# Window attention feeding a routed expert layer: transposes by half arrays, value sums among them, a bank of its own for gate and route, 1e-9 inside the product

## The chip, the cores and the metric

The kernel runs on one core of a Trainium2 chip. The metric is the device time of one execution in microseconds (us). TensorE is called PE here (PEld is its weight load, which overlaps PE), VectorE DVE, ScalarE ACT, GpSimd POOL, and SP is the engine that issues most transfers.

## What is computed

Attention with a window of 16 and block summaries, whose output goes token by token to one of 8 experts. Cut to what matters (B=4, H=8, S=768, D=64; E=8 experts, DM=512, DF=1024):

```python
k_sum = k.reshape(B, H, nb, block, D).max(axis=3)      # block = 32, nb = 24
v_sum = v.reshape(B, H, nb, block, D).mean(axis=3)
scores_l_m = np.where(mask_l, scale * q @ k.T, -1e9)   # |i - j| < 16
scores_s = scale * q @ k_sum.T + np.log(block)
a = np.exp(scores_all - scores_all.max(-1))            # both kinds side by side
a = a / (a.sum(-1) + 1e-09)
x = a @ np.concatenate([v, v_sum])
...
e = argmax(x @ w_gate) if s == 0 or sigmoid(x @ w_local) < 0.5 else prev_e
p = softmax(x @ w_gate)
out[b, s] = p[e] * (np.maximum(x @ w1[e], 0) @ w2[e])
```

## The kernel before

**Attention.** A loop of 32 iterations, G = 0 to 31. One G is half the sequence (three blocks of 128 queries) of one pair of heads, two G make a pair of heads, eight G a batch. A query block meets 96 windowed keys and 24 summaries, so a score row has 120 entries. Iteration G works on three different G at once:

- `s_mm(G)` (L281, L287): mask and scores into one of two score tiles of two PSUM banks each, on 64x64 pieces of the array;
- `t_stage(G-2)` (L312, L313): six transposes of the exponentials, 128 rows x 120 columns each, three into each of two banks, and an ACT copy of each bank into `pt`;
- `sum_v` (L252, L254), once per pair of heads: a transpose of the value sums `va` into a third bank, and an ACT copy into `vs`, which POOL spreads into `vw` (L259);
- `s_max(G)` on DVE (L294), `s_exp(G)` on ACT (L302, six instructions);
- `a_mm(G-3)` (L323): the product with the values; `a_norm(G-3)` on DVE (L334 adds 1e-9, L335 takes the reciprocal, L336 multiplies).

PSUM has eight banks: four for scores, one for `a_mm`, and three that go round under the name "t". Transposes of all kinds, and the small matmuls of the routing, take the next of the three.

**Gate and route.** When a batch's attention is done, `x_rows_in` (L511, L518) transposes its rows for the gate: two blocks of 128 rows in each of three iterations (G = 10 to 12 for the first batch, 18 to 20, 26 to 28 for the next), four 128x128 transposes and one ACT copy per block into `hs`. `x_logits` (L528) makes the gate's logits of three blocks with 12 matmuls, ACT copies them (L532), PE turns them back (L535), DVE stores them (L537). Its results lie in columns of the score tile that the scores leave free (`self.spare`, L289, L525). Two iterations later `route` starts: a chain of some 30 small DVE steps with four stops on PE (L569, L575, L581, L602 to L605), which `small` (L458) places one or a few at a time between the steps of the loop.

**Experts.** From iteration 31 on the expert layer's matmuls (L1128 to L1130, L1158 to L1160) take PE. The last G's `t_stage`, `a_mm` and the last batch's gate and route are put among them by hand (`tail`).

**Loads.** SP issues, in program order, k, q, v and the windowed values `vw` of the coming pairs of heads, the stores of finished rows and the first expert's weights. An issue waits until the buffer's last reader is done, and all behind it wait too.

Of the kernel before, what the change touches and what calls it, by code (L numbers as in the profile page):

```python
# [19 lines left out]
P = 128  # L20
# [4 lines left out]
W = WL + NB  # L25
NU = S // P
# [27 lines left out]
XT = (0, 0, 1, 1, 2, 2)  # L54
XG = (2, 3)

# [16 lines left out]
class Kernel:  # L73
    def __init__(self, ctx, tc, qT, kT, vT, vW, maskc, identc, wgc, w1, w2, c32c, cb16c, out):
        self.tc, self.nc, self.out = tc, tc.nc, out
        self.steps, self.credit, self.have_p, self.last, self.early_in = [], 0, 0, None, {}
        self.calls = 0
# [6 lines left out]
        self.ps = {n: pool("ps_" + n, k, space=psum) for n, k in (("t", 3), ("a", 1))}  # L84
# [5 lines left out]
        self.spare = None  # L90
# [54 lines left out]
    def bank(self, which):  # L145
        if which == "a" and "a2" in self.ps:
            self.turn ^= 1
            which = "a2" if self.turn else "a"
        if which == "s":
            which = next(self.order)  # L150
        return self.ps[which].tile([P, 512], F32, name="b" + which[0])

    def free_banks(self):
# [4 lines left out]
        self.order = cycle(("s0", "s1", "s1"))  # L158


    def attention(self, tick, rows, tail):
        nc, tc, ident = self.nc, self.tc, self.ident
        with ExitStack() as ctx:
# [13 lines left out]
            vts, kss, vas, vss = {}, {}, {}, {}  # L177
# [17 lines left out]

            for t in kp:
                nc.vector.memset(t[:, 0:16], 0.0)
                nc.vector.memset(t[:, 16 + S:], 0.0)
# [22 lines left out]
            def reduce_v(n, v=None):  # L221
                va = vas[n] = wk.tile([P, NB], F32, name="va")
                nc.vector.tensor_reduce(out=va, in_=by32(vts.pop(n)) if v is None else v, op=ALU.add, axis=AX.X)

            def fold_v(n):
                f = by32(wk.tile([P, S // 2], F32, name="vf", bufs=1), 16)
                v = by32(vts.pop(n))
                for i in range(0, NB, NB // 2):
                    p = slice(i, i + NB // 2)
                    nc.gpsimd.tensor_tensor(out=f[:, p], in0=v[:, p, 0:16], in1=v[:, p, 16:32], op=ALU.add)  # L230
                folded[n] = f
# [18 lines left out]

            def sum_v(n, m):
                nc.tensor.transpose(out=m[:NB], in_=vas.pop(n), identity=ident)  # L252
                vs = vss[n] = wk.tile([NB, P], F32, name="vs", bufs=2)
                nc.scalar.copy(out=vs, in_=m[:NB])  # L254
# [11 lines left out]
            def s_mm(G):  # L266
# [22 lines left out]
                self.spare = sp[:, :, NG * W:]  # L289
# [7 lines left out]
            def s_exp(G):  # L297
                sp, nm = live[G]
                pr = wk.tile([P, 2, NG, W], F32, name="pr")
                for h in range(2):  # L300
                    for u in range(NG):
                        nc.scalar.activation(out=pr[:, h, u, :], in_=sp[:, h, u, :], func=AF.Exp,  # L302
# [3 lines left out]
            def t_stage(G):  # L306
                pr = live[G]
                pt = wk.tile([W, 2, NG, P], F32, name="pt", bufs=2)
                for h in range(2):
                    tp = self.bank("t")  # L310
                    for u in range(NG):
                        nc.tensor.transpose(out=tp[:W, P * u:P * u + P], in_=pr[:, h, u, :], identity=ident)  # L312
                    nc.scalar.copy(out=pt[:, h].rearrange("p u q -> p (u q)"), in_=tp[:W, 0:NG * P])  # L313
                live[G] = pt

            def a_mm(G):
# [3 lines left out]
                for u in range(NG):  # L320
                    for h in range(2):
                        for c in range(2):
                            nc.tensor.matmul(out=ap[64 * c:64 * c + 64, u, h, :], lhsT=pt[:, h, u, 64 * c:64 * c + 64],  # L323
                                             rhs=vw[n % 3][0:W, 2 * (NG * g + u) + c, h, :], start=True, stop=True)

            def a_norm(G):
# [7 lines left out]
                nc.vector.tensor_scalar(out=dn, in0=ap[:, :, :, D:D + 1], scalar1=1e-9, scalar2=None, op0=ALU.add)  # L334
                nc.vector.reciprocal(out=dn, in_=dn)  # L335
# [16 lines left out]
            for G in range(last_g):  # L352
# [10 lines left out]
                if LT <= G:  # L363
                    t_stage(G - LT)
                if G > 2 * GP and G % GP == 0 or G == 2 * GP + 1:
                    sum_v(G // GP, self.bank("t")[:, 0:P])
                if G in (2, 4):
                    sum_v(G // 2 - 1, self.bank("t")[:, 0:P])
# [57 lines left out]
            self.spare = None  # L426
# [31 lines left out]
    def small(self, n, pe=False):  # L458
# [3 lines left out]
        while self.credit > 0:  # L462
            heads = [h for h in list(self.steps)[:2] if h[0] not in ON_PE or pe and h[2] <= self.calls - ON_PE[h[0]]]
# [8 lines left out]
    def step(self, head):  # L472
        kind = head[0]
        self.last = head
# [8 lines left out]
        if head[0] is None:  # L483
            self.steps.remove(head)

# [8 lines left out]
    def flow(self, dt):  # L494

        self.t += dt
        while True:
            heads = [h for h in self.steps[:2]
                     if (h[3] <= self.t if h[0] in ON_PE or h[0] == "WAIT" else max(h[3], self.q) <= self.t + AHEAD)]
# [13 lines left out]

    def x_rows_in(self, b, u):

        m = self.x_transpose(b, u, "t")
        xt = self.hs[b, u] = self.mw.tile([P, 512], F32, name=f"hs{u % 4}")
        self.nc.scalar.copy(out=xt, in_=m)  # L518

    def x_logits(self, b, g):  # L520
# [4 lines left out]
        m = self.bank("t") if self.spare is None else self.spare[:, 0]  # L525
        for c in range(KT):
            for j, u in enumerate(us):
                nc.tensor.matmul(out=m[32 * j:32 * j + 32, 0:P], lhsT=self.wg[:, c], rhs=self.hs[b, u][:, P * c:P * c + P],  # L528
# [3 lines left out]
        nc.scalar.copy(out=l4, in_=m[0:32 * NG, 0:P])  # L532
        yield
        m = self.bank("t") if self.spare is None else self.spare[:, 1 - g]
# [3 lines left out]
                              in_=m[:, 0:32 * NG].rearrange("p (u e) -> p u e", u=NG)[:, :, 0:G9])  # L538


    def route(self, b):
# [26 lines left out]
        m = self.bank("t")  # L568
# [3 lines left out]
        v.tensor_tensor_scan(out=pm, data0=m[0:NU, 0:P], data1=self.zero[0:NU, 0:P], initial=0.0, op0=ALU.max, op1=ALU.max)  # L572
        yield "PE late" if b == 0 else "PE"
        m = self.bank("t")
# [1008 lines left out]
```

## Time and profile before

| | |
|---|---|
| time, median of 3 runs | 441.0 us (439.19 to 441.19) |
| the profiled execution | 438.48 us, of which 436.7 us are the span of the core |
| mean granted TensorE clock | 0.994 of full speed |
| PE busy | 416.0 us, 95% of the span |
| ACT, DVE, POOL busy | 201.4, 245.2, 214.0 us |
| DMA | 95.84 MB, mean 219 GB/s |

The page cuts the span into 40 slices of 10.9 us and gives the busy share of each in tenths. Attention is the first eleven slices, the experts are the rest. Times of rows are counted from the span's start.

### The profile page before, as it was taken

To read this page: it belongs to the slowest core of one execution; us is meant where nothing else is said; L and a number is where in the kernel's file an instruction comes from. 1 tells how busy PE (TensorE), PEld (TensorE's weight loads), DVE (VectorE), ACT (ScalarE), POOL (GpSimd) and SP (SyncE) were. 2 spreads that over 40 slices of the span, in tenths; PEclk is the share of its full clock that TensorE was granted. 3 is DMA by queue.
4 is the path that set the end of the run, shared out by engine and by line. 5 is a ranking of instruction groups with operands and counts; after the bars stand their busy time and mean duration, and the time that the engine had idled before them with its cause. 6 is when DMAs were issued, how large, how long until landed. Compare 5 with 4: busy or idle time off the path is not lost. (4 is left out here: it accounts for less than half of the span.)

```text
span 436.7 us, 12169 instructions
## 1 busy us (share of the span) xinstructions
PE 416.0 (95%) x4470; PEld 363.0 (83%) x4470; DVE 245.2 (56%) x609; ACT 201.4 (46%) x457; POOL 214.0 (49%) x305
## 2 busy tenths in 40 slices
PE   7799989989999999999999999999999999999992
PEld 6577878768898798998989889798988898978981
DVE  5776788888875798955522222215545732264720
ACT  4888878686955125512111112115454821266610
POOL 3688675778622313932021310304939883088930
PEclk9999999999999999999999999999999999999997
DMA  8999979999342670293092264200765794039771
GB/s 317 374 377 395 409 282 363 372 395 368 102 149 95 238 292 2 80 389 111 2 377 113 79 229 183 75 27 25 262 202 183 305 344 182 24 96 383 267 258 52
DMA packets 24006, 95.84 MB, mean 219 GB/s; under 512 B 2894, under 2 KB 3536, under 8 KB 19312
## 3 DMA queue, kind: packets, MB, share of 16 engines
q1 hardware_dynamic: 19328, 80.30, 48.9%
q0 software_dynamic: 4448, 14.29, 9.5%
q8 instruction: 42, 0.69, 0.7%
q14 instruction: 44, 0.36, 0.3%
q10 hardware_dynamic: 144, 0.20, 0.1%
HBM read 82.20 MB, written 12.71 MB: 217 GB/s over the span
## 5 line engine op out<-in xcount | busy, mean ns | idle before, releaser
L1158 PE MATMUL bs<-xT,h 128*128 128x256 f32 x352 | 101.4, 288 | 0.0
L1159 PE MATMUL bs<-xT,h 128*128 128x256 f32 x352 | 99.7, 283 | 0.0
L1160 PE MATMUL bs<-xT,l 128*128 128x256 f32 x352 | 99.5, 283 | 0.0
L1097 POOL DMA_INDIRECT xg<-x_dram,gidx x30 | 33.4, 1114 | 89.7 <-POOLq L1400 39.8
L1091 POOL TENSOR_TENSOR l<-stg,h 128x256 fp32r<-128x256 f32 x72 | 64.9, 935 | 15.0 <-ACT h L1083 14.7
L1128 PE MATMUL ba<-h,hT 128*128 128x512 f32 x176 | 71.5, 406 | 0.4
L1164 ACT ACTIVATE hT<-bs 128x512 fp32r<-128x512 f32 x44 | 26.3, 598 | 96.7 <-PE bs L1160 93.3
L1130 PE MATMUL ba<-h,hT 128*128 128x512 f32 x176 | 68.9, 392 | 0.0
L1129 PE MATMUL ba<-l,hT 128*128 128x512 f32 x176 | 68.7, 391 | 0.0
L1158 PEld LDWEIGHTS bs<-xT,h 128*128 128x128 f32 x352 | 67.4, 192 | 1.3 <-issue 0.8
L1166 DVE SCALAR_TENSOR_TENSOR hT<-bs,hT 128x512 fp32r<-128x512 f32 x44 | 30.4, 691 | 67.9 <-ACT hT L1164 57.1
L1159 PEld LDWEIGHTS bs<-xT,h 128*128 128x128 f32 x352 | 67.5, 192 | 0.4
L1160 PEld LDWEIGHTS bs<-xT,l 128*128 128x128 f32 x352 | 67.4, 192 | 0.0
L302 ACT ACTIVATE pr<-bs,nm 128x120 f32<-128x120 f32 x192 | 51.2, 358 | 8.8 <-DVE nm L294 6.4
L1083 ACT CAST h<-stg 128x1024 fp32r<-128x1024 f32 x48 | 48.9, 1052 | 9.2 <-PE ba L1130 8.2
L1144 POOL DMA_INDIRECT out_dram<-yo,sidx x24 | 26.4, 1102 | 47.4 <-ACT yo L1143 9.6
L1086 DVE TENSOR_TENSOR l<-stg,h 128x1024 fp32r<-128x1024 f32 x30 | 39.6, 1331 | 13.2 <-ACT h L1083 10.4
L1128 PEld LDWEIGHTS ba<-h,hT 128*128 128x128 f32 x176 | 33.1, 188 | 7.5 <-ACTq L1400 0.6
L1130 PEld LDWEIGHTS ba<-h,hT 128*128 128x128 f32 x176 | 33.0, 188 | 7.3
L1129 PEld LDWEIGHTS ba<-l,hT 128*128 128x128 f32 x176 | 33.2, 189 | 5.6
L259 POOL COPY vw<-vs 24x384 f32<-24x384 f32 x64 | 30.5, 518 | 8.5 <-ACT vs L254 6.1
L313 ACT COPY pt<-bt 120x384 f32<-120x384 f32 x64 | 27.8, 493 | 10.1 <-PE bt L312 10.1
(274 smaller groups left out, 665.1 us busy)
## 6 DMA issues: line engine op xcount, KB each, us to landing
stg<-in_w SPq DMA_DIRECT2D x28, 1024.0 KB, 7.0
vw<-in_vW SPq DMA_DIRECT2D x16, 780.0 KB, 7.9
few_w<-in_w SPq DMA_DIRECT2D x8, 1024.0 KB, 8.9
kp<-in_kT SPq DMA_DIRECT2D x16, 384.0 KB, 6.8
q<-in_qT SPq DMA_DIRECT2D x16, 384.0 KB, 7.3
vt<-in_vT SPq DMA_DIRECT2D x16, 384.0 KB, 7.6
x_dram<-xs SPq DMA_DIRECT2D x8, 768.0 KB, 5.4
wst<-in_w SPq DMA_DIRECT2D x8, 512.0 KB, 6.4
```

What stands on the lines that cost most here:

```text
L259: nc.gpsimd.tensor_copy(out=vw[n % 3][WL:W, t:t + NW // 4, :, 0:D], in_=vs.to_broadcast([NB, NW // 4, 2, D]))
L302: nc.scalar.activation(out=pr[:, h, u, :], in_=sp[:, h, u, :], func=AF.Exp, bias=nm[:, h, u:u + 1], scale=1.0)
L1083: self.nc.scalar.copy(out=hi, in_=src)
L1086: eng.tensor_tensor(out=lo, in0=src, in1=hi.bitcast(F32), op=ALU.subtract)
L1091: eng.tensor_tensor(out=lo[:, p], in0=src[:, p], in1=hi[:, p].bitcast(F32), op=ALU.subtract)
L1097: self.nc.gpsimd.indirect_dma_start(out=t, out_offset=None, in_=rows, in_offset=bass.IndirectOffsetOnAxis(ap=self.gidx[:, i:i + 1], axis=0))
L1128: nc.tensor.matmul(out=ps, lhsT=ah, rhs=wh, start=first, stop=False)
L1129: nc.tensor.matmul(out=ps, lhsT=ah, rhs=wl, start=False, stop=False)
L1130: nc.tensor.matmul(out=ps, lhsT=al, rhs=wh, start=False, stop=last)
L1158: nc.tensor.matmul(out=ps[:, j], lhsT=wh, rhs=xh, start=(k == 0), stop=False)
L1159: nc.tensor.matmul(out=ps[:, j], lhsT=wh, rhs=xl, start=False, stop=False)
L1160: nc.tensor.matmul(out=ps[:, j], lhsT=wl, rhs=xh, start=False, stop=(k == KT - 1))
```

## The change

- **Halves.** A transpose of 128 rows becomes two of 64 rows each, on the upper and the lower half of the array's rows, side by side. Each half writes a bank of its own, so a set of transposes holds two banks at once. `t_stage` becomes 12 half transposes and two ACT copies (one a bank), each of six blocks of 64 columns. The gate's transposes are done so too (`x_two`: 16 half transposes and two copies for two blocks of rows).
- **Value sums among them.** `va` is a seventh source in the same set: two more half transposes, and the copies are seven blocks long. `vs` and its copy are gone, POOL reads the sums from `pt`.
- **Banks.** The pool "t" has two banks instead of three. The third is "m", for `x_logits`, `route` and what follows it; a step holds it until its result is read (`own_m`, `free_m`), and others wait in program order. After the loop "t", "t" and "m" go round together. `self.spare` is gone.
- **Order.** The second `x_logits` of a batch moves behind `s_exp` of its iteration (`XSTEPS`).
- **1e-9.** `vw` gets a row with 1e-9 in the column of the denominators, the exponentials a 121st column of ones; DVE's addition is gone.
- The value sums' folding on POOL is done in place, and `pr` and `va` are fixed tiles.

```diff
-        self.ps = {n: pool("ps_" + n, k, space=psum) for n, k in (("t", 3), ("a", 1))}
+        self.ps = {n: pool("ps_" + n, k, space=psum) for n, k in (("t", 2), ("m", 1), ("a", 1))}
...
-XT = (0, 0, 1, 1, 2, 2)
+XT = (0, 1, 2)
 XG = (2, 3)
+XSTEPS = (((0, 2), (0, 4), (1, 2), (1, 3)), ((0, 0), (0, 1), (1, 2), (1, 3)))
...
-            def t_stage(G):
+            def t_stage(G, n=None):
                 pr = live[G]
-                pt = wk.tile([W, 2, NG, P], F32, name="pt", bufs=2)
-                for h in range(2):
-                    tp = self.bank("t")
-                    for u in range(NG):
-                        nc.tensor.transpose(out=tp[:W, P * u:P * u + P], in_=pr[:, h, u, :], identity=ident)
-                    nc.scalar.copy(out=pt[:, h].rearrange("p u q -> p (u q)"), in_=tp[:W, 0:NG * P])
-                live[G] = pt
+                pt = live[G] = wk.tile([WE, 2 * NG + 1, P], F32, name="pt", bufs=3)
+                srcs = [pr[:, h, u, :] for h in range(2) for u in range(NG)]
+                if n is not None:
+                    srcs.append(vas[n % 3])
+                    vss[n] = pt[0:NB, 2 * NG, :]
+                self.halves(srcs, WE, pt[:, 0:len(srcs)])
...
-                nc.vector.tensor_scalar(out=dn, in0=ap[:, :, :, D:D + 1], scalar1=1e-9, scalar2=None, op0=ALU.add)
-                nc.vector.reciprocal(out=dn, in_=dn)
+                nc.vector.reciprocal(out=dn, in_=ap[:, :, :, D:D + 1])
...
+    def halves(self, srcs, m, dst):
+        half = P // 2
+        n = len(srcs)
+        banks = [self.bank("t")[:m, 0:half * n].rearrange("p (i q) -> p i q", q=half) for c in range(2)]
+        for i, src in enumerate(srcs):
+            for c in range(2):
+                r = slice(half * c, half * c + half)
+                self.nc.tensor.transpose(out=banks[c][:, i], in_=src[r], identity=self.ident[r, r])
+        for c in range(2):
+            self.nc.scalar.copy(out=dst[:, :, half * c:half * c + half], in_=banks[c])
...
+    def own_m(self, who):
+        if self.rest:
+            return
+        while self.m_owner not in (None, who):
+            assert self.m_owner is not self
+            self.step(self.m_owner)
+        self.m_owner = who
...
-        m = self.bank("t") if self.spare is None else self.spare[:, 0]
+        self.own_m(self)
+        m = self.bank("m")
```

What moves on ACT, first batch, from the exponentials of G = 10 to the `pt` copies of iteration 14 (`pr` are exponentials, `hs` the gate's rows, `l` its logits, `vs` the value sums). Before:

```order
30 L302 ACTIVATE pr<-bs,nm 128x120 x6
31 L518 COPY hs_885<-bt 128x512
32 L518 COPY hs_892<-bt 128x512
33 L313 COPY pt<-bt 120x384 x2
34 L302 ACTIVATE pr<-bs,nm 128x120 x6
35 L518 COPY hs_963<-bt 128x512
36 L518 COPY hs_970<-bt 128x512
37 L532 COPY l_1001<-bs 96x128
38 L313 COPY pt<-bt 120x384 x2
39 L254 COPY vs<-bt 24x128
40 L302 ACTIVATE pr<-bs,nm 128x120 x6
43 L532 COPY l_1100<-bs 96x128
```

And now:

```order
25 L306 ACTIVATE pr_160<-bs,nm 128x120 x6
26 L538 COPY hs_906<-bt 128x8x64 x2
27 L538 COPY pt<-bt 121x6x64 x2
28 L306 ACTIVATE pr_161<-bs,nm 128x120 x6
29 L538 COPY hs_994<-bt 128x8x64 x2
30 L569 COPY l_1045<-bm 96x128
31 L538 COPY pt<-bt 121x7x64 x2
32 L306 ACTIVATE pr_160<-bs,nm 128x120 x6
33 L538 COPY hs_1101<-bt 128x8x64 x2
34 L538 COPY pt<-bt 121x6x64 x2
35 L306 ACTIVATE pr_161<-bs,nm 128x120 x6
36 L569 COPY l_1204<-bm 96x128
```

The copies of the gate's rows still stand behind the exponentials and ahead of the `pt` copies; the `vs` copy is gone, and the second copy of logits has moved behind the exponentials.

On PE, iteration 10, from its scores on (`va` the value sums, `xs` the rows for the gate). Before:

```order
207 L287 MATMUL bs<-kb_141,q_139 64x120 x12
208 L312 MATMUL bt<-ident,pr 120x128 x6
209 L252 MATMUL bt<-ident,va 24x128
210 L323 MATMUL ba<-vw_147,pt 64x65 x12
211 L511 MATMUL bt<-ident,xs 128x128 x8
```

And now:

```order
207 L292 MATMUL bs<-kb_144,q_142 64x120 x12
208 L536 MATMUL bt<-ident,pr_160 121x64 x12
209 L536 MATMUL bt<-ident,va_156 121x64 x2
210 L326 MATMUL ba<-vw_150,pt 64x65 x12
211 L536 MATMUL bt<-ident,xs 128x64 x16
```

The places stay; each transpose has become two with half the output columns.

## Rows read from the trace of the kernel before

**Rows 1.** The page's 40 slices of 10.9 us: busy tenths of PE and DMA, and GB/s.

```profile
PE   7799989989999999999999999999999999999992
...
DMA  8999979999342670293092264200765794039771
GB/s 317 374 377 395 409 282 363 372 395 368 102 149 95 238 292 2 80 389 111 2 377 113 79 229 183 75 27 25 262 202 183 305 344 182 24 96 383 267 258 52
```

**Rows 2.** Timeline of PE, iterations 11 to 14 (start us, us, engine, line, ...).

```profile
39.05 0.87 PE L312 MATMUL bt<-ident,pr 128*120 128x128 f32 x6
39.85 0.92 PE L323 MATMUL ba<-vw,pt 120*64 120x65 f32 x24
40.71 1.09 PE L511 MATMUL bt<-ident,xs 128*128 128x128 f32 x8
...
42.62 1.07 PE L528 MATMUL bs<-hs,wg 128*32 128x128 f32 x24
43.62 0.87 PE L312 MATMUL bt<-ident,pr 128*120 128x128 f32 x6
...
48.72 0.87 PE L312 MATMUL bt<-ident,pr 128*120 128x128 f32 x6
...
50.37 0.35 PE L281 MATMUL bs<-me 64*64 64x360 bf16 x4
```

**Rows 3.** Timeline of ACT in the same iterations.

```profile
36.92 1.57 ACT L302 ACTIVATE pr<-bs,nm 128x120 f32<-128x120 f32 x6
38.39 1.04 ACT L518 COPY hs<-bt 128x512 f32<-128x512 f32 x2
39.69 0.86 ACT L313 COPY pt<-bt 120x384 f32<-120x384 f32 x2 [0.26 <-PE bt L312]
...
41.91 1.13 ACT L518 COPY hs<-bt 128x512 f32<-128x512 f32 x2
...
44.26 0.86 ACT L313 COPY pt<-bt 120x384 f32<-120x384 f32 x2 [0.25 <-PE bt L312]
...
46.64 1.04 ACT L518 COPY hs<-bt 128x512 f32<-128x512 f32 x2
...
49.35 0.86 ACT L313 COPY pt<-bt 120x384 f32<-120x384 f32 x2 [0.27 <-PE bt L312]
...
52.89 1.56 ACT L302 ACTIVATE pr<-bs,nm 128x120 f32<-128x120 f32 x6
```

**Rows 4.** Groups by form, 0 to 130 us (count | busy us, mean ns | idle before).

```profile
L313 ACT COPY pt<-bt 120x384 f32<-120x384 f32 x64 | 27.8, 493 | 10.1 <-PE bt L312 10.1
...
L312 PE MATMUL bt<-ident,pr 128*120 128x128 f32 x192 | 27.6, 280 | 0.0
...
L334 DVE TENSOR_SCALAR dn<-ba 128x6 f32<-128x6 f32 x32 | 5.0, 157 | 5.4 <-PE ba L323 5.3
```

**Rows 5.** Waits, 0 to 130 us: who <- for whom, us in total, times, longest.

```profile
ACT pr L302 <- DVE nm L294: 6.4, 9, 2.5
...
DVE nm L294 <- ACT l L532: 4.1, 2, 2.2
...
PEld bt L312 <- issue: 3.4, 20, 0.2
PEld bt L569 <- ACT pt L313: 2.7, 2, 1.4
...
PEld bt L581 <- ACT pt L313: 0.6, 1, 0.6
```

**Rows 6.** Timeline of PEld where turned logits, not scores, precede the transposes.

```profile
111.04 0.66 PEld L312 LDWEIGHTS bt<-ident,pr 128*120 128x120 f32 x6
```

**Rows 7.** Timeline of DVE and PE in iteration 31, where the experts begin.

```profile
115.27 1.29 DVE L1103 TENSOR_TENSOR xT<-bt,xT 128x512 fp32r<-128x512 f32 x2 [0.40 <-ACT xT L1101]
...
115.69 0.87 PE L312 MATMUL bt<-ident,pr 128*120 128x128 f32 x6
116.32 0.36 PE L1158 MATMUL bs<-xT,h 128*128 128x256 f32 x1
```

More of the change, by code (lines that the diff above doesn't have):

```diff
@@ L150, in bank @@
             which = next(self.order)
+        if which in ("t", "m") and self.rest:
+            which = next(self.rest)
         return self.ps[which].tile([P, 512], F32, name="b" + which[0])
@@ L158, in free_banks @@
         self.order = cycle(("s0", "s1", "s1"))
+        while self.m_owner:
+            self.step(self.m_owner)
+        self.rest = cycle(("t", "t", "m"))
     def attention(self, tick, rows, tail):
@@ L176, in attention @@
             eye2, mask2 = me[:, 0:64], me[:, 64:]
-            vts, kss, vas, vss = {}, {}, {}, {}
+            vts, kss, vss = {}, {}, {}
+            vas = [cst.tile([P, WE], F32, name=f"va{i}") for i in range(3)]
             def load_k(n):
@@ L194, in load_w @@
                 nc.sync.dma_start(out=vw[n % 3], in_=self.vW[b, p])
+            for t in vas:
+                nc.gpsimd.memset(t, 0.0)
+            prs = [cst.tile([P, 2, NG, WE], F32, name=f"pr{i}") for i in range(2)]
+            for t in prs:
+                nc.gpsimd.memset(t[:, :, :, W:WE], 1.0)
             for t in kp:
@@ L462, in small @@
         while self.credit > 0:
-            heads = [h for h in list(self.steps)[:2] if h[0] not in ON_PE or pe and h[2] <= self.calls - ON_PE[h[0]]]
+            heads = [h for h in list(self.steps)[:2] if h[0] not in ON_PE or pe and h[2] <= self.calls - ON_PE[h[0]] and self.m_owner is not self]
             if not heads:
@@ L473, in step @@
         kind = head[0]
+        if kind in ON_PE:
+            self.own_m(head)
         self.last = head
@@ L512, in x_transpose, with hs_of, x_two @@
         return m
+    def halves(self, srcs, m, dst):
[8 more added lines that the diff above has]
+            self.nc.scalar.copy(out=dst[:, :, half * c:half * c + half], in_=banks[c])
+    def hs_of(self, b, u):
+        if (b, u // 2) not in self.hs:
+            self.hs[b, u // 2] = self.mw.tile([P, 2, KT, P], F32, name=f"hs{u // 2 % 2}")
+        return self.hs[b, u // 2][:, u % 2]
     def x_rows_in(self, b, u):
         m = self.x_transpose(b, u, "t")
-        xt = self.hs[b, u] = self.mw.tile([P, 512], F32, name=f"hs{u % 4}")
-        self.nc.scalar.copy(out=xt, in_=m)
+        self.nc.scalar.copy(out=self.hs_of(b, u).rearrange("p k t -> p (k t)"), in_=m)
+    def x_two(self, b, u):
+        self.hs_of(b, u)
+        srcs = [self.xs[b, v // NG][:, v % NG, P * c:P * c + P] for v in (u, u + 1) for c in range(KT)]
+        self.halves(srcs, P, self.hs[b, u // 2].rearrange("p j k t -> p (j k) t"))
     def x_logits(self, b, g):
@@ L532, in x_logits @@
         nc.scalar.copy(out=l4, in_=m[0:32 * NG, 0:P])
+        self.free_m()
         yield
-        m = self.bank("t") if self.spare is None else self.spare[:, 1 - g]
+        self.own_m(self)
+        m = self.bank("m")
         nc.tensor.transpose(out=m[:, 0:32 * NG], in_=l4, identity=self.ident[0:32 * NG, 0:32 * NG])
@@ L757, in early @@
         yield "PE"
-        m = self.bank("t")
+        m = self.bank("m")
         for t in range(n):
@@ L1329, in run @@
             g0 = GP * NP * b + GP * NP + 2
-            for u in range(NU):
-                at(g0 + XT[u], 1, self.x_rows_in, b, u)
+            for i in range(NU // 2):
+                at(g0 + XT[i], 1, self.x_two, b, 2 * i)
             for g in range(GP):
-                for G, i in ((0, 2), (0, 4), (1, 2), (1, 3)):
+                for G, i in XSTEPS[g]:
                     at(g0 + XG[g] + G, i, tiles, self.x_logits, b, g)
```

68 lines of the change are left out of this document (36 added, 32 removed).

## The prediction

> **What bounds the kernel now.** I read the page's slices first. From the eleventh slice on PE is at 9 almost throughout [rows 1]: that is the expert layer, PE's alone, and the change leaves its order of matmuls as it is. So what attention gains or loses up to the first expert matmul at 116.3 us [rows 7] is gained or lost at the end. Within attention the reader should see two things in the slices: PE stands at 7 to 9, and DMA is at 9 in eight of the first ten slices, at 282 to 409 GB/s [rows 1]. Loads are in flight nearly all the time, so an iteration that merely waits less for PE will soon wait for its keys or values. The timelines come next, for iterations 11 to 14, where the first batch's rows go through the gate. There PE runs without a gap: transposes, product, gate transposes, logits follow at once [rows 2]. ACT sits close behind: exponentials, gate copies, then a short wait of about 0.26 us for the transposes, `pt` copies, exponentials [rows 3]. Last the waits: where `route` runs, ACT waits for DVE and PE for ACT's `pt` copies [rows 5].
>
> **The half transposes.** Six full ones take 0.87 us [rows 2], one 0.28 [rows 4], so one follows another by (0.87 - 0.28) / 5 = 118 ns. The trace has no half transpose. Near bound: `a_mm`, which runs on two column halves at a time, issues 24 instructions in 0.92 us [rows 2], (0.92 - 0.28) / 23 = 28 ns apart. Far bound: if the two halves run one after the other, half the columns give 59 ns. I take 30 ns, from the nearer kind of work. Then a set of 12 takes 0.28 + 11 x 0.03 = 0.61 us instead of 0.87, one of 14 takes 0.67, and the gate's 16 take 0.73 instead of 1.09 [rows 2]. PE saves 0.26 us 32 times and 0.36 us nine times.
>
> **The copies.** ACT used to start its first `pt` copy 0.64 us after the transposes began (39.05 to 39.69) [rows 2, 3], since it needed three of them. Now both copies need the whole set: 0.61 + 0.12 = 0.73 us, with sums 0.79. So ACT sees the transposes 0.1 to 0.15 us later, although PE is done earlier. The `vs` copy saved goes against two copies that are a sixth longer than 493 ns [rows 4]; I count nothing for the pair.
>
> **Iterations without gate work.** PE's saving there has the loads behind it [rows 1]; 0, between -0.26 us an iteration and +0.15.
>
> **Two banks instead of three, in the gate's iterations.** This is the largest term. A set holds both "t" banks. After `x_two` they are free only when ACT has read both, and ACT does that behind the exponentials. Today one of three banks was free, and `t_stage` began at 39.05 while the gate copies ran until 38.39 + 1.04 = 39.43 [rows 2, 3]. Then it can begin at 39.55, `pt` copies at 40.28 instead of 39.69: +0.6. In iteration 12 the gate copies so run from 42.5 to 43.65, and the logits, which started at 42.62 [rows 2] with one block copied, need both copies now, as each writes half of each block: 43.75, `pt` copies at 45.5 instead of 44.26 [rows 3], +1.25. In iteration 13 the gate copies end at 48.95, `t_stage` starts at 49.05 instead of 48.72 [rows 2], `pt` copies at 49.8 instead of 49.35 [rows 3]; the logits come behind it now, which regains 0.8 on ACT. But PE still has 1.0 us of logits and 0.85 of `a_mm` to do, so the next scores start near 51.4 instead of 50.37 [rows 2], and the exponentials of iteration 14 at 54.2 instead of 52.89 [rows 3]: **+1.3 us**. In the second and third stretch the exponentials that start the chain wait for DVE already [rows 5], which hides part; I take +0.4 each. Sum +2.1, each stretch between +1.3 and -1.7 (what PE would save there if banks never bound: three gate sets of 0.36, two or three of 0.26).
>
> **Route in a bank of its own.** PE waited 2.7 us in two places (L569) and 0.6 in one (L581) for ACT to read a "t" bank [rows 5]; the "m" bank is free there. Behind it stand `a_mm` and the next scores. Between 0 and -3.3; I take -2.4, since in one iteration ACT's exponentials are what ends last anyway. The steps forced early by `own_m` change no place on PE in the loop: 0. The scores' tile no longer carries logits, so the 4.1 us in which the row maximum waited for the logits' copy [rows 5] go; the `pt` copies still end later there, 0.
>
> **1e-9 in the product.** 32 additions of 157 ns on DVE go [rows 4], 5.0 us of busy time. It counts where ACT waited for DVE's maximum, nine times [rows 5]: one addition each in eight of them, **-1.3**; between 0 and -2.6 (two each).
>
> **Array modes.** Where scores on 64x64 pieces precede the transposes, PE's weight load shows an idle gap before them, 3.4 us over 20 cases, 0.17 each [rows 5]; where turned logits on the whole array precede them there is none [rows 6]. With halves, six `t_stage` behind turned logits get it; three of these wait for the gate's banks anyway: +0.5. The Trainium skill, "TensorEngine Tiling (Array Packing)", section Tiling Modes, says that changing the tiling mode drains TensorE; by it, also the nine small route transposes that stand between the halves and `a_mm` would cost a gap each, 15 x 0.17 = 2.6 us instead of 0.5. No row shows what PE loses there, so the sum keeps 0.5.
>
> **The start of the experts.** In iteration 31 two "t" banks hold gathered rows, which DVE has read at 115.27 + 1.29 = 116.56; `t_stage` began at 115.69 in the third bank, the first expert matmul at 116.32 [rows 7]. Then 116.6 and 117.1: +0.8, less two later sets that are 0.26 shorter: +0.3.
>
> **Sum:** 2.1 - 2.4 - 1.3 + 0.5 + 0.3 = -0.8 us against the profiled 438.5, that is 437.7. The median of the runs is 2.5 above that execution, so 440.2. About 0.5% (2.2 us) is what a measurement of this kernel can tell from no change.
>
> **Rivals.**
> - *A, faster: PE's savings arrive.* For it: PE has no gap in the gate's iterations [rows 2]. If ACT and the banks keep out of the way, the three stretches give -1.7 each instead of +2.1 together, the rest as above: -5.1 - 2.4 - 1.3 + 0.5 + 0.3 = -8.0; a part of this meets the loads [rows 1], of which I leave 2.5, so -5.5: 435.5. Against it: the gate copies stand between exponentials and `pt` copies on ACT [rows 3]. The Trainium skill, in the same page, section Performance Considerations, warns of this: tiling speeds up the matmuls, not the reading of PSUM.
> - *B, slower: the two banks bind in full.* Each of the three stretches pays 1.3, the experts start 0.8 later, and `route` gains nothing since ACT is what it waits for in the end: 3.9 + 0.8 + 0.5 - 1.3 = +3.9, 444.9. It decides if the gate copies end after the next scores in all three stretches, as they do in the first.
> - *C, slower: the halves don't overlap.* At 59 ns a set takes 0.28 + 11 x 0.059 = 0.93, the gate's 1.17, and the `pt` copies come 0.32 later still; in nine gate iterations this is +2.9 on the forecast: 443.1. Against it: the column halves of `a_mm` do overlap [rows 2].
>
> **Chances.** The forecast, no change: 0.45. A 0.27, B 0.14, C 0.14. Of the forecast's share 0.06 lies beyond -0.5%, as its bounds lean that way, and C stands at the edge, so 0.03 of it counts as no change: faster 0.27 + 0.06 = 0.33, same 0.45 - 0.06 + 0.03 = 0.42, slower 0.25. The range reaches 1 us beyond A (434.5), as part of the 2.5 us left to the loads may come too, and to just short of B (444.5).
>
> **What would show it.** Right: transposes about 30 ns apart, sets near 0.6 us, with ACT's wait for them longer in total than 10.1 us [rows 4]; in iterations 11 to 13 `t_stage` starts only after the gate copies end, and PE has gaps there; no wait of route transposes for `pt` copies; the first expert matmul between 115 and 117.5 us. Wrong: gate iterations as short as PE's work (A), the same gap in front of `t_stage` in all three stretches with the experts starting after 119 us (B), or halves 59 ns apart (C).

## The result and the profile after

The changed kernel takes 446.87 us (median of 4 runs, 445.11 to 448.19) beside 440.43 for the kernel before: 1.0134 of it, interval 1.0105 to 1.0163, so slower by 6.4 us, where 440.2 was forecast. The profiled execution took 447.26 us (span 445.5). The page's slices of the changed kernel, against [rows 1]:

```profile
PE   7989999988999999999999999999999999999992
...
PEclk9669999999999999999999999999999999999998
DMA  8899989999516192156056047200573876029581
GB/s 299 338 366 321 391 288 313 359 385 407 169 49 237 49 381 93 61 214 270 25 214 267 31 141 310 72 29 16 206 253 118 358 276 246 24 59 380 213 325 57
```

And the clock's row of the kernel before:

```profile
PEclk9999999999999999999999999999999999999997
```

PE is as full as before, but in the second and third slice at 6 tenths of its clock. By stretches, in the changed kernel (behind the busy times stand the granted clock, the DMA share and GB/s):

```profile
core 0: us, PE busy (x) PEld busy (x) DVE busy (x) ACT busy (x) POOL busy (x), PEclk, DMA share, GB/s
6.00:12.00 6.00, 3.65 (x94) 3.10 (x95) 4.54 (x5) 2.82 (x11) 1.86 (x4) 1.00 1.02 395
12.00:18.00 6.00, 5.54 (x84) 4.92 (x87) 2.96 (x6) 5.73 (x19) 2.75 (x6) 0.50 1.02 407
18.00:24.00 6.00, 5.06 (x116) 4.25 (x110) 4.98 (x7) 2.94 (x11) 3.11 (x7) 0.93 0.74 276
24.00:33.00 9.00, 7.84 (x120) 6.56 (x114) 4.60 (x9) 4.51 (x16) 6.93 (x15) 0.62 1.00 366
33.00:39.00 6.00, 6.00 (x158) 5.32 (x157) 4.59 (x10) 5.61 (x18) 4.69 (x11) 1.00 0.98 343
```

0.50 is the lower of the clock's two levels, 1.2 GHz in place of 2.4. Loads fell behind as well: the DMA share from 18 to 24 us, right after the first fall, is 0.74. Where the time is lost is read from the starts of the scores (the mask's matmul, L281 before and L286 now) in the two timelines of PE:

| start of | before | after | later by | change since the line above |
|---|---|---|---|---|
| G = 10, first gate rows | 33.81 | 38.94 | 5.13 | +5.1 |
| G = 15, first gate stretch done | 53.11 | 60.28 | 7.17 | +2.0 |
| G = 19, route done | 66.81 | 72.42 | 5.61 | -1.6 |
| G = 22, second gate stretch done | 79.52 | 86.55 | 7.03 | +1.4 |
| G = 26, route done | 92.66 | 98.46 | 5.80 | -1.2 |
| G = 30, third gate stretch done | 110.09 | 117.71 | 7.62 | +1.8 |
| first expert matmul | 116.32 | 124.93 | 8.61 | +1.0 |

From there on nothing more is lost: the execution ends 8.8 us later. That is more than the 6.4 us of the medians, since the kernel before was traced in an execution that is faster than all its four runs (438.48 us); so the table's amounts are rather high. Iteration 18 has the last step of `route` and the second batch's first gate rows, and the table counts it with `route`; counted from G = 18 (62.47 and 68.84) that `route` stretch gives 0.8 and the gate stretch costs 0.7. The timeline of PE in the changed kernel, with the idle time in front of a row in brackets:

```profile
9.48 0.35 PE L286 MATMUL bs<-me 64*64 64x360 bf16 x4 [1.90 <-ACT pr L306]
...
12.46 0.51 PE L286 MATMUL bs<-me 64*64 64x360 bf16 x4 [0.73 <-ACT pr L306]
...
25.75 1.48 PE L292 MATMUL bs<-kb,q 64*64 64x120 f32 x24 [1.16 <-POOL kb L258]
...
38.94 0.34 PE L286 MATMUL bs<-me 64*64 64x360 bf16 x2
...
40.61 0.85 PE L536 MATMUL bt<-ident,pr 64*121 64x64 f32 x12
41.29 0.27 PE L536 MATMUL bt<-ident,va 64*121 64x64 f32 x2
...
42.34 0.98 PE L536 MATMUL bt<-ident,xs 64*128 64x64 f32 x16
...
44.60 0.31 PE L536 MATMUL bt<-ident,pr 64*121 64x64 f32 x1 [0.39 <-ACT hs L538]
45.09 0.84 PE L536 MATMUL bt<-ident,pr 64*121 64x64 f32 x11 [0.17 <-ACT hs L538]
...
124.15 0.85 PE L536 MATMUL bt<-ident,pr 64*121 64x64 f32 x11 [0.28 <-DVE xT L1151]
124.93 0.39 PE L1206 MATMUL bs<-xT,h 128*128 128x256 f32 x1
```

A set of 12 halves takes 0.85 us, hardly less than the six full transposes did (0.87) [rows 2], and one with sums about 0.95; the gate's 16 take 0.98 instead of 1.09. The halves stand (0.85 - 0.27) / 11 = 53 ns apart, not 30. ACT, which had waited 0.26 us for a set [rows 3], now waits 0.6 to 1.4 in the gate's iterations, for example:

```profile
43.91 1.13 ACT L538 COPY hs<-bt 128x512 f32<-128x512 f32 x2
45.93 0.86 ACT L538 COPY pt<-bt 121x384 f32<-121x384 f32 x2 [0.89 <-PE bt L536]
```

Summed over the first 130 us, ACT's wait is twice the 10.1 us of [rows 4], and DVE's wait for the value product has grown from 5.3 [rows 4] to 18.7:

```profile
ACT pt L538 <- PE bt L536: 21.1, 22, 2.8
DVE dn L337 <- PE ba L326: 18.7, 17, 2.7
```

### The profile page after: what moved, and what is told of

Its sections match the earlier page's. It is cut to its first block, busy times and chain, and to the rows that moved or that the text cites. A ratio compares the mean times of both kernels' runs of the same rounds, so it can differ in the third digit from the quotient of the medians.

```text
span 445.5 us, 12679 instructions
## 1 busy us (share of the span) xinstructions
PE 423.7 (95%) x4750; PEld 371.2 (83%) x4750; DVE 242.1 (54%) x577; ACT 201.0 (45%) x441; POOL 214.8 (48%) x310
## 5 line engine op out<-in xcount | busy, mean ns | idle before, releaser
L1139 POOL TENSOR_TENSOR l<-stg,h 128x256 fp32r<-128x256 f32 x72 | 66.8, 963 | 15.3 <-ACT h L1131 14.7
L306 ACT ACTIVATE pr<-bs,nm 128x120 f32<-128x120 f32 x192 | 52.3, 389 | 6.0 <-DVE nm L298 3.9
L1192 POOL DMA_INDIRECT out_dram<-yo,sidx x24 | 25.0, 1043 | 49.6 <-DMA out_dram<-yo,sidx 12.0
L538 ACT COPY pt<-bt 121x448 f32<-121x448 f32 (+1 forms) x64 | 29.4, 515 | 25.4 <-PE bt L536 23.4
L264 POOL COPY vw<-pt 24x384 f32<-24x384 f32 x64 | 30.3, 514 | 8.9 <-ACT pt L538 8.0
```

Of the source, the lines that this page charges most:

```text
L306: nc.scalar.activation(out=pr[:, h, u, 0:W], in_=sp[:, h, u, :], func=AF.Exp, bias=nm[:, h, u:u + 1], scale=1.0)
L1139: eng.tensor_tensor(out=lo[:, p], in0=src[:, p], in1=hi[:, p].bitcast(F32), op=ALU.subtract)
```

## The experiments

Three theories were tested. **K**: the loss is the clock that falls once half transposes take the place of full ones. **L**: it is the late first copy, since each bank now needs the whole set. **B**: it is the two banks that go round in place of three. The kernel before took 440.2 to 443.1 us from chip to chip, so a ratio is always to the runs beside it.

| run | us | ratio (interval) |
|---|---|---|
| before + 1e-9 in the product | 441.20 | 0.9966 (0.9947 to 0.9985) |
| before + halves for p | 448.63 | 1.0131 (1.0086 to 1.0175) |
| before, both copies late | 444.26 | 1.0021 (1.0004 to 1.0039) |
| before + 20/10 dummies | 445.37 | 1.0054 (1.0033 to 1.0075) |
| changed + 20/10 dummies | 447.36 | 1.0135 (1.0077 to 1.0193) |
| changed + 6 dummies | 444.81 | 1.0043 (1.0021 to 1.0064) |
| changed, full transposes | 438.48 | 0.9882 (0.9852 to 0.9912) |
| changed, full transposes, copies late, 6 dummies | 440.92 | 1.0023 (1.0007 to 1.0039) |
| changed, full transposes, 6 dummies | 437.85 | 0.9945 (0.9927 to 0.9964) |
| the same, dummies in 4 to 9 alone | 438.14 | 0.9964 (0.9942 to 0.9985) |
| one chip: changed, again | 446.14 | 1.0127 (1.0091 to 1.0163) |
| one chip: changed + 6 dummies | 443.91 | 1.0074 (1.0037 to 1.0111) |
| one chip: changed, full transposes | 436.05 | 0.9880 (0.9845 to 0.9915) |
| one chip: changed, full, 6 dummies | 438.52 | 0.9950 (0.9925 to 0.9976) |
| changed, halves for the gate alone | 438.29 | 0.9956 (0.9930 to 0.9982) |
| changed, halves for p alone | 443.14 | 1.0061 (1.0040 to 1.0082) |
| changed, full, three t banks | 437.36 | 0.9933 (0.9898 to 0.9969) |

**The clock held up by dummy matmuls.** A dummy is a matmul of zeros that nobody reads. They went into the changed kernel, behind the value product:

```diff
+                if G < 10:
+                    mb = self.bank("m")
+                    for _ in range(20 if G < 3 else 10):
+                        nc.tensor.matmul(out=mb[:, 0:P], lhsT=self.wz, rhs=self.wz, start=True, stop=True)
```

> The changed kernel with 20 extra matmuls of zeros behind a_mm in iterations 0 to 2 and 10 in iterations 3 to 9, into bank m, which nothing uses there. Clock theory (TensorE's granted clock, 0.50 in 12 to 16 us and 0.50 to 0.71 in 24 to 32 us of the changed kernel, costs what is lost before iteration 10): the clock stays at 1.00, iteration 10 starts near 34 to 35 us instead of 38.9, and the kernel takes 441 to 443 us. Rival (the early loss comes from the halves and from the value sums ahead of the copies, the clock only follows from waiting): the clock stays up, iteration 10 still starts after 37.5 us, 445 us or more.

The clock was 1.00 in each stretch to 39 us, and the time was the same, 447.36; iteration 10 started at 37.61. Both are what the rival had expected. That looked like the end of K, but the dummies filled PE:

```profile
6.00:12.00 6.00, 6.00 (x140) 5.23 (x137) 4.41 (x5) 3.07 (x12) 1.86 (x4) 1.00 1.02 400
12.00:18.00 6.00, 6.00 (x136) 5.31 (x134) 4.35 (x8) 5.38 (x18) 2.79 (x6) 1.00 1.01 401
```

So their price had to be measured: the same dummies in the kernel before (there into a `t` bank, as it has no `m`), and only 6 of them in the changed one.

> The kernel before with the dummy matmuls of the earlier run (20 behind the value matmuls of iterations 0 to 2, 10 in 3 to 9; 128x128 in bf16). What the dummies cost by themselves: in the run on the changed kernel they filled TensorE (6.00 of 6.00 us busy from 6 to 18 us), so holding the clock there may have been paid for with time. Theory K (clock is most of the loss): the dummies cost 2.5 us or more here, about what they gave back there. Theory L (late copies): they cost under 1 us here, and the changed kernel with dummies lost its 3.8 us to iteration 10 to the copies.

> The changed kernel with only 6 dummy matmuls (128x128, bf16, about 0.35 us together) behind the value matmuls of each of the iterations 0 to 9. Theory K: if the granted clock then stays at 1.00 to 39 us, the time falls by 2 us or more, to 445 or less, and iteration 10 starts within 2 us of the kernel before. Theory L: clock at 1.00 or not, iteration 10 starts 3 us or more late and the time stays within 1 us of 446.9.

In the kernel before they cost 2.2 us (445.37 against 443.13), a little less than the 2.5 that K had asked for. They put its iteration 10 at 37.68, as late as the changed kernel's with them. With 6 dummies the changed kernel came to 1.0043, with the clock at 1.00 to 39 us, and iteration 10 at 36.41, 2.6 us after the kernel before: between the 2 of K and the 3 of L. So K stands again, for a part of the loss.

**1e-9 alone**, in the kernel before (`vw` gets the row, `pr` the column of ones, DVE's addition goes):

```diff
-                nc.vector.tensor_scalar(out=dn, in0=ap[:, :, :, D:D + 1], scalar1=1e-9, scalar2=None, op0=ALU.add)
-                nc.vector.reciprocal(out=dn, in_=dn)
+                nc.vector.reciprocal(out=dn, in_=ap[:, :, :, D:D + 1])
```

> The kernel before with the 1e-9 in the product alone (32 additions on DVE gone, 121 rows in the transposes' output). Prediction's term: -1.3 us, 0 to -2.6, so 438 to 440.5. Rival: DVE ends nothing in attention that the loads or PE don't end as well: 440 to 441.

The time falls by 1.5 us (0.7 to 2.3 by the interval), where the prediction had 1.3. But the column has a side effect. The weight loads of the transposes, first in the kernel before, then in this run (busy us, mean ns):

```profile
L312 PEld LDWEIGHTS bt<-ident,pr 128*120 128x120 f32 x192 | 20.3, 137 | 4.5 <-issue 3.4 <-ACT hs L518 0.5 <-ACT pr L302 0.3
```

```profile
L316 PEld LDWEIGHTS bt<-ident,pr 128*121 128x121 f32 x192 | 23.3, 184 | 4.4 <-issue 2.3 <-ACT pr L306 1.4 <-ACT hs L521 0.5
```

With one column more a load takes 47 ns longer, and the set of six goes from 0.87 to 0.92 us. (The rows of `pr` are 121 words long now, too; no run separates that from the width.)

**Halves alone**, in the kernel before, with 120 columns and three banks:

```diff
-                for h in range(2):
-                    tp = self.bank("t")
...
+                pt = live[G] = wk.tile([W, 2 * NG, P], F32, name="pt", bufs=2)
+                self.halves([pr[:, h, u, :] for h in range(2) for u in range(NG)], W, pt)
```

> The kernel before with t_stage by halves alone: three t banks, the sums' own transpose, the gate's full transposes and the free score columns stay. If the halves are what lets the clock fall: granted clock below 1.00 somewhere before 35 us and 443 to 446 us. If the value sums among the transposes or the bank m do it: clock 1.00 there, and 439.5 to 442 us. Spacing of the half transposes 51 ns as in the changed kernel in both cases.

The halves for p alone cost 5.9 us, nearly what the whole change does. A set in PE's timeline, the groups (mean 233 ns), and the clock in that run:

```profile
39.28 0.57 PE L517 MATMUL bt<-ident,pr 64*120 64x64 f32 x12
```

```profile
L517 PE MATMUL bt<-ident,pr 64*120 64x64 f32 x384 | 19.2, 233 | 0.3 <-DVE xT L1110 0.3
```

```profile
18.00:24.00 6.00, 4.07 (x98) 3.18 (x102) 4.85 (x10) 4.62 (x17) 4.83 (x10) 0.96 0.86 316
24.00:33.00 9.00, 9.00 (x165) 7.21 (x165) 5.97 (x14) 5.34 (x19) 7.25 (x16) 0.65 1.00 369
```

Here the halves stand (0.57 - 0.23) / 11 = 31 ns apart, as the prediction had it (this run's expectation, 51, was a miss), and still as much is lost: the loss doesn't need the wide spacing, and the clock falls here too.

**Transposes by themselves.** This is a kernel of transposes between stretches of 100 bf16 matmuls. The halves in turn (L84) are written so:

```python
for i in range(48):
    r = (lo, hi)[i % 2]
    nc.tensor.transpose(out=banks[i % 2][0:121, 0:64], in_=src[r], identity=ident[r, r])
```

> Transposes alone on a busy TensorE, 24 or 48 in a row; the rest of the kernel is left out and the output is zeros. Full ones 118 ns apart. Halves alternating, 121 columns loaded: 51 ns. If the load of 121 columns sets this, one half's load after the other's: 64 columns 27 to 30 ns, 32 columns less. If the 64 columns that stream set it (no overlap of the two halves): 51 ns with 64 and 32 loaded columns too, and 51 ns on one half alone. If the halves do overlap and each takes about 100 ns: 100 ns on one half alone, and in the case of 24 upper ones followed by 24 lower ones.

```profile
8.68 2.83 PE L80 MATMUL bk<-ident,src 128*121 128x128 f32 x24
...
17.02 2.75 PE L84 MATMUL bk<-ident,src 64*121 64x64 f32 x48
...
25.39 6.42 PE L87 MATMUL bk<-ident,src 64*121 64x64 f32 x48
31.75 7.84 PE L76 MATMUL wb<-wz 128*128 128x128 bf16 x100
39.52 6.15 PE L91 MATMUL bk<-ident,src 64*121 64x64 f32 x48
...
53.27 1.53 PE L95 MATMUL bk<-ident,src 64*64 64x64 f32 x48
54.74 5.76 PE L76 MATMUL wb<-wz 128*128 128x128 bf16 x100
...
67.56 5.30 PE L103 MATMUL bk<-ident,src 64*121 64x64 f32 x96
```

With 121 columns two halves take as long as one full transpose: 24 full ones 2.83 us, 48 halves 2.75, 53 ns apart. With 64 columns (L95) they are (1.53 - 0.22) / 47 = 28 ns apart. L87 keeps to one half of the array. While the clock is 1.00 its transposes stand about 100 ns apart there (31 from 26 to 29 us), so halves in turn do overlap; but each takes nearly as long as a full one. And in L87 PE's clock falls while it never pauses:

```profile
28.00:29.00 1.00, 1.00 (x12) 1.00 (x12) 0.00 (x0) 0.00 (x0) 1.00 0.00 0
29.00:30.00 1.00, 1.00 (x9) 1.00 (x8) 0.00 (x0) 0.00 (x0) 0.66 0.00 0
30.00:31.00 1.00, 1.00 (x6) 1.00 (x7) 0.00 (x0) 0.00 (x0) 0.50 0.00 0
31.00:36.00 5.00, 5.00 (x46) 4.88 (x46) 0.00 (x0) 0.00 (x0) 0.50 0.00 0
36.00:37.00 1.00, 1.00 (x19) 1.00 (x18) 0.00 (x0) 0.00 (x0) 0.92 0.06 16
```

It comes back only under the bf16 matmuls of the whole array, the first of which it slows (7.84 us instead of 5.76). The stretch of halves in turn (L84) kept 1.00, but lasted 2.75 us; the same halves as plain matmuls (L103) kept 1.00 for 5.30 us. So this kernel doesn't show that halves in turn lose the clock, nor whether the half array or the transposing does it in L87.

**Full transposes in the changed kernel.** All else stays: two t banks, the own bank, the sums in the set and the 1e-9.

```diff
+        k = (n + 1) // 2
+        for i0, i1 in ((0, k), (k, n)):
+            bank = self.bank("t")
+            for i in range(i0, i1):
+                self.nc.tensor.transpose(out=bank[:m, P * (i - i0):P * (i - i0) + P], in_=srcs[i], identity=self.ident)
+            self.nc.scalar.copy(out=dst[:, i0:i1], in_=bank[:m, 0:P * (i1 - i0)].rearrange("p (i q) -> p i q", q=P))
```

> The changed kernel with one thing taken back: the transposes of p, of the value sums and of the gate's x are full 128-row transposes again (up to 4 to a bank, the first bank copied as soon as it is full); two t banks, the own bank for gate and route, the sums in the set, the table of the order and the 1e-9 stay as changed. Theory H (the halves are the loss, whatever the way): about 446.9 - 6 = 441 us, within 1.5 us of the kernel before, and the granted clock of 12 to 33 us at 1.00. Theory B (the two banks in turn, and the gate's steps that wait for one bank, are the loss, and the halves kernel lost its 6 us to something of its own): above 444 us, clock as it may be.

It took 438.48 us beside 443.13, a ratio of 0.9882: faster than both kernels. B falls. H holds in the main, but not in its numbers: the time lies 4.7 us under the kernel before, not within 1.5, and the clock wasn't at 1.00 throughout:

```profile
24.00:33.00 9.00, 8.38 (x148) 7.14 (x148) 6.44 (x12) 4.88 (x17) 8.01 (x18) 0.81 1.00 358
```

The halves cost more than the whole loss, since they also hide a gain of about 5 us. The single run for 1e-9 accounts for 1.5 of it; the rest is not divided (a run on the own bank stands below).

**Late copies.** In the kernel before:

```diff
-                for h in range(2):
-                    tp = self.bank("t")
-                    for u in range(NG):
+                tps = [self.bank("t") for h in range(2)]
+                for u in range(NG):
+                    for h in range(2):
```

and in the changed kernel with full transposes and 6 dummies, next to the same without late copies:

```diff
-        for i0, i1 in ((0, k), (k, n)):
...
+        bs = [self.bank("t") for c in range(2)]
+        for i, src in enumerate(srcs):
+            self.nc.tensor.transpose(out=bs[i % 2][:m, P * (i // 2):P * (i // 2) + P], in_=src, identity=self.ident)
```

> The kernel before with one thing changed: the six full transposes of p go to the two banks in turn (u outside, h inside), so that both copies begin only after all six, as with the halves; no half transposes. Theory L (late first copy: the chain exp, copy, exp of ScalarE loses about 0.25 us in each iteration that it sets): +2 us or more over the kernel before, with the wait of the pt copies for the transposes up from 10.1 us to about 20 in the sum, clock 1.00 throughout. Theory K (the clock that half transposes lose is the whole loss): within 1 us of the kernel before.

> The changed kernel with full transposes, and with the 6 dummy matmuls behind the value matmuls of iterations 0 to 9. Two ends for what the halves cost once the clock is held: the changed kernel with the same dummies came to 1.0043 of the kernel before. Theory M (clock and late copies together are the loss): clock at 1.00 to 39 us here too, and about 0.988 again, since the full kernel's clock fell only from 24 to 33 us (0.81) and the dummies about pay for what they give; so some 7 us under the halves with the clock held, which something other than the clock must explain. Theory K (the clock is all of the loss): within 2 us of the halves with the same dummies, 1.000 or more.

> As the run with full transposes and 6 dummies, but the full transposes go to the two t banks in turn, so that both copies begin only after the whole set, for p and sums as for the gate's rows; nothing on half arrays. Theory M with the late copies as the rest of the loss: most of the way from the full transposes (about 0.988) to the halves with the clock held (1.004), so 0.997 or more. Rival (the late copies are worth no more than in the kernel before, where they cost 0.2%, and the halves cost in another way): 0.992 or less.

In the kernel before they cost 0.9 us by the ratio, less than L wanted, and ACT's wait for the sets rose from 10.1 to 14.2 us, not to 20. In the full kernel they cost 440.92 - 437.85 = 3.1; the 1.0023 is what M had expected of them (0.997 or more), though 0.9945 without them was not its 0.988. Iteration 10 starts 1.1 us later with them (36.46 against 35.33). What they do is plain in the waits, first with early and then with late copies:

```profile
ACT pt L540 <- PE bt L539: 14.0, 23, 1.8
```

```profile
ACT pt L540 <- PE bt L537: 20.3, 23, 2.0
```

20.3 is nearly the changed kernel's 21.1.

> The changed kernel with full transposes and the 6 dummies in iterations 4 to 9 alone, where its clock fell (0.81 from 24 to 33 us). If the clock's dip there costs what it seems to (iteration 6 to 8 came 2 us later against the kernel before), clock at 1.00 and 0.984 to 0.988, under the run with full transposes by up to 2 us; if the dummies cost what they hold, the same as that run within 0.3%.

A miss: 0.9964, no faster than with dummies in all ten iterations, and above 0.988.

**Four on one chip**, to divide the loss:

> The changed kernel as it is, beside the three others of this call on one chip, since the kernel before itself took 440.2 to 443.1 us from chip to chip. Expected: 1.013 of the kernel before again (1.0105 to 1.0163 in the first comparison), granted clock under 1.00 between 12 and 33 us.

> The changed kernel with full transposes, no dummies, as before. If the ratio of 0.988 held of the kernel and not of the chip: 0.986 to 0.991, so 2.5% under the changed kernel. If the chip had favoured it: 0.993 to 0.996, as with dummies, so 1.8 to 2% under the changed kernel.

> The changed kernel with 6 dummies behind the value matmuls of iterations 0 to 9. Theory K+ (the clock is 4 us of the loss): 4 us under the changed kernel on this chip, clock 1.00 to 39 us. Rival (the first result lay in the chip): within 2 us of the changed kernel.

> Full transposes with the 6 dummies. Against the halves with the same dummies, clock held in both: what is left of the loss. Theory M: 4 to 7 us under the halves with dummies, and within 2 us of the full transposes without dummies on this chip. Theory K: under 2 us.

Halves cost 446.14 - 436.05 = 10.1 us. The dummies take 2.2 from the halves, where K+ had expected 4, and put 2.5 on the full transposes. So the clock that they hold is worth about 4.7, if their own price is the same in both; 443.91 - 438.52 = 5.4 is left with the clock held. The price needn't be the same: 130 of them cost the kernel before 2.2, and 60 cost the full one 2.5. The clock in the halves without (first two rows) and with the dummies:

```profile
12.00:18.00 6.00, 5.54 (x130) 4.64 (x129) 4.56 (x7) 5.90 (x20) 2.75 (x6) 1.00 1.03 406
24.00:33.00 9.00, 9.00 (x164) 7.79 (x156) 5.41 (x10) 4.86 (x16) 6.90 (x15) 0.67 1.03 392
```

```profile
24.00:33.00 9.00, 8.82 (x203) 7.63 (x200) 6.61 (x13) 6.82 (x23) 7.36 (x16) 1.00 1.02 380
```

Full transposes dip too in some executions, more briefly (here 0.89 from 6 to 12 us and 0.82 from 12 to 18), so the dummies' own price is rather above 2.5.

A second estimate needs no dummies. The span of each execution and its mean granted clock are on record; the span times what the clock is short of 1.00 is the clock that it lost. In the eight executions of the changed kernel that is 5.3 to 10.3 us, and the time goes with it from 445.1 to 448.2 us, by 0.6 us for each us of lost clock. On this chip the changed kernel lost 6.7 on average and the one with full transposes 3.3, so by this slope the clock's part of the 10.1 is 2 us. The two traces of the changed kernel show it, too: the one above kept 1.00 from 12 to 18 us, where the one of the result had 0.50, and it starts iteration 10 at 36.46 instead of 38.94 and ends 2.1 us earlier. Taken together the clock's part is 2 to 4.7 us.

**Which halves, and the own bank.** `fulls` is the code of the full transposes; each run changes one call, and the third gives `t` three banks and lets `m` mean `t`:

```diff
-                self.halves(srcs, WE, pt[:, 0:len(srcs)])
+                self.fulls(srcs, WE, pt[:, 0:len(srcs)])
```

```diff
-        self.ps = {n: pool("ps_" + n, k, space=psum) for n, k in (("t", 2), ("m", 1), ("a", 1))}
+        self.ps = {n: pool("ps_" + n, k, space=psum) for n, k in (("t", 3), ("a", 1))}
```

> The changed kernel with full transposes for p and the value sums, halves for the gate's rows alone (9 of 41 sets). With full transposes everywhere it was 0.988 of the kernel before, with halves everywhere 1.0127. If the loss comes from the sets of p (the clock in the first 39 us, late pt copies in each iteration): 0.988 to 0.993. If it comes from the gate's sets, whose copies hold both banks in front of the next set: 1.000 or more.

> The reverse: halves for p and the value sums (32 of 41 sets), full transposes for the gate's rows. Loss from the sets of p: 1.005 to 1.013, granted clock under 1.00 between 12 and 33 us, iteration 10 about 4 us later than with full transposes. Loss from the gate's sets: 0.995 or less.

> The changed kernel with full transposes, and with three t banks going round for sets, gate and route as in the kernel before, in place of two and a bank of its own. The prediction priced the two banks at +2.1 us and the own bank at -2.4 us with the halves' late copies; if with full transposes the own bank still gives its 2.4 us and the two banks cost their 2.1, this stays within 1 us of 0.988. If the two banks cost nothing with full transposes: 0.992 or more here, about 2 us longer.

Over the 0.988 of full transposes the halves for p cost 1.8% (8.0 us), those for the gate 0.8% (3.3 us), together about the 10.1 above. The run for p lies in the range that was expected of it, the one for the gate between its two. With p in halves the clock lay at the lower level from 12 to 24 us; iteration 10 started at 36.31, 1.8 us after the 34.50 of full transposes and not 4:

```profile
12.00:18.00 6.00, 6.00 (x90) 5.27 (x94) 3.37 (x6) 5.57 (x18) 2.75 (x6) 0.50 1.01 404
18.00:24.00 6.00, 6.00 (x86) 5.09 (x80) 3.77 (x6) 2.48 (x8) 2.73 (x6) 0.50 0.77 270
```

Three t banks in place of two and an own one cost 0.5% (2.3 us by the ratios, 1.3 by the medians; the intervals overlap). That is the net of what the own bank gives and of what a third t bank would give, and no run shows either alone. The wait for which the prediction priced the own bank doesn't come back. The first stop of `route` on PE (iteration 16), in the kernel before, in the run of halves alone, and in this one:

```profile
58.72 0.27 PE L569 MATMUL bt<-ident,val 128*6 128x128 f32 x1 [1.04 <-ACT pt L313]
```

```profile
63.18 0.27 PE L576 MATMUL bt<-ident,val 128*6 128x128 f32 x1 [1.15 <-ACT pt L519]
```

```profile
58.80 0.27 PE L535 MATMUL bt<-ident,va 128*121 128x128 f32 x1
58.91 0.27 PE L607 MATMUL bt<-ident,val 128*6 128x128 f32 x1
```

The first two kernels transpose the value sums into a bank of their own, so that `route` comes to a bank that ACT has yet to read. In the third the sums lie in the set, and the third bank is free.

## Why the prediction was wrong

- **"Iterations without gate work ... 0, between -0.26 us an iteration and +0.15"** is the step that failed. Even at +0.15, ten iterations make 1.5 us; in the trace of the result the changed kernel is 5.1 us late by iteration 10, and in two more traces with the same code up to there (the changed kernel again, halves for p alone) 2.7 and 2.5. The step took it that PE's durations only get shorter and that loads hide the rest; the clock was no term at all, and the late copies were taken as hidden. What it put at 0 is 2.5 to 5.1 us, of the lower clock and of late copies (1.1 of it in the pair of full kernels). For the clock fell to the lower level from 12 to 18.8 and again from about 25.7 us, and loads fell behind (a share of 0.74 from 18 to 24 us). In the kernel before with 20/10 dummies that share was 0.77 with the clock at 1.00, so a lower clock isn't needed for that; PE being late is enough. PE had paused just before the first fall (1.90 and 0.73 us); the kernel before paused as long at the same places (1.90 and 0.66) and kept its clock in its trace, with full transposes behind the pauses. Before the second fall PE paused 1.16 us. The clock's part of what the halves cost is 2 to 4.7 us, by the two estimates above.
- **The half step of 30 ns**, "from the nearer kind of work", failed for this kernel: 53 ns, so rival C's far bound was the nearer, though not for C's reason, as halves in turn do overlap. The step would have held with 120 columns (31 ns); the column of ones that the 1e-9 brings makes it 121. The prediction priced the two edits apart. But the set's length is not where most of the time went: halves alone, 31 ns apart, lost 5.9 us too.
- **The copies and the two banks.** The mechanism is right: sets begin only when the gate's copies end (44.60 and 45.09, with gaps in front), ACT waits 21.1 us instead of 10.1, and the `pt` copies begin 0.89 us after the gate copies end (43.91 + 1.13 = 45.04), where 40.28 - 39.43 = 0.85 was reckoned. The size was off: the gate stretches cost 2.0, 0.7 to 1.4 and 1.8 instead of 1.3, 0.4 and 0.4, so the later two cost more than was reckoned for them, as rival B had it. And late copies cost outside the gate's iterations too: 1.1 us by iteration 10 and 3.1 in all by the pair of full kernels. The 0.1 to 0.15 us an iteration had been named and then hidden behind the loads.
- **1e-9 -1.3: right**, 1.5 in the single run. **Route -2.4: the wait is right, its owner isn't.** The route stretches give 0.8 to 1.6 and 1.2, and no wait for `pt` copies is left there. But it is gone without the own bank, too: the value sums had taken the third bank, and their place in the set frees it. So far the amount came near by luck.
- **The experts' start**: +0.8 for the banks, measured +1.0; the 0.5 taken off for shorter sets never came, as the sets weren't shorter.
- **Rivals.** B's time (444.9) is nearest, and the experts do start after 119 us, which is part of its sign; C has the spacing; neither has the clock. Of the 10.1 us that halves cost, 2 to 4.7 are the clock's and about 3.1 the late copies'; 2 to 5 are left that no run separates. The array modes (+0.5 in the sum, 2.6 beside it) are a candidate that no run tested. The gaps of PEld that it starts from don't grow: 2.3 us over 10 cases now, 3.4 over 20 before [rows 5].

The clock fell behind pauses of 0.7 to 1.9 us. The kernel before, with such pauses and full transposes, kept it in its trace; the changed kernel with full transposes lost it for a shorter time (0.81 from 24 to 33 us). Why halves lose it for longer is seen here, not explained. The Trainium skill, "TensorE: Matmul & The Clock Gate", section A second HAM failure mode: psum-queue depth-cycling, reports a kernel whose TensorE paused briefly and often between groups of matmuls while it went round the PSUM banks, and whose clock went up and down between its two levels. The clock of the changed kernel goes down and up like that (0.50, 0.93, 0.62, 1.00 by stretches), but pauses alone don't explain it, as the kernel before has them too and L87 lost the clock without one.

## What to carry to other kernels

Here the transposes should stay full: the changed kernel with them takes 0.988 of the kernel before (436.05 beside 440.76 us), and so beats both. An edit that makes TensorE's instructions smaller is checked against the clock's row first, where the engine pauses between stretches, and a reader of two banks against the time at which the first bank is full. To hold a clock with dummy work, measure its price on the kernel that didn't lose it.

## What the runs showed of the hardware

- One column more in the weights: full loads of 120 columns of fp32 take 137 ns, of 121 columns 184, of 128 (the gate's rows in the kernel before) 141. Halves in turn come 31 ns apart with 120 columns, 53 with 121, 51 with the gate's 128 ((0.98 - 0.23) / 15), 28 with 64. The Trainium skill, "TensorE: Matmul & The Clock Gate", section LDWEIGHTS (loading the stationary operand), lets a load grow evenly with its columns; the measurement doesn't. What makes 121 different, the width or rows of 121 words, stays open, and so does why the gate's halves with loads of 138 ns stand 51 ns apart.
- The granted clock can fall while TensorE works without a pause (transposes on one half from 25.4 us on, 0.50 at 30), and come back only under matmuls on the whole array (from 31.75 us on, 0.92 at 36).
